# Batches 4 to 7: q transposed in 32x32 blocks by VectorE and moved by DMA, in place of TensorE transposes

## Chip, cores, metric

One core of a Trainium2 chip. The metric is the device time of one execution, in microseconds (us). A ratio is the mean time of one kernel's fast runs over that of the other's of the same rounds, so it is not quite the ratio of the medians quoted beside it.

## The reference, cut to what matters

```python
# attention without a score matrix; q, k, v: (8 batches, 8 heads, 576, 64)
q_s = softmax(q, axis=-1);  k_s = softmax(k, axis=2)
kv  = einsum('bhsd,bhse->bhde', k_s, v)
x   = einsum('bhsd,bhde->bhse', q_s, kv)       # -> (4608 tokens, 512)
# GEGLU block, d_ff = 1536
out = (gelu(x @ w_gate) * (x @ w_val)) @ w_out
```

## The kernel before

Per batch, TensorE runs the FFN of batch b (12 steps of four gate and four value matmuls, then four output tiles of twelve matmuls), and between these it prepares batch b+1. To multiply q by kv, q must lie with its features on the partitions, so it is transposed on TensorE into PSUM and copied back by VectorE. 512 of a batch's 576 tokens go through the FFN as one batch; the 64 left over of every batch are collected in `xtr` and run as a ninth, "left-over" batch between batches 6 and 7.

The names in the profile lines: `eq` is the exponential of q; `pst` and `pstr` are its transposes in PSUM (the memory that TensorE writes its results to), `eqt` the transposed q; `pskv` is the key-value product; `psx` and `psxr` are the products of kv with q for the 512 tokens and for the 64 left over, copied to `xt` and `xtr`; `psg` and `psv` are the results of the gate and value matmuls, `ht` is their gated product, `psy` an output tile.

```python
def unit_t(b, g, eng="dve"):                 # 8 transposes for two head pairs, 1 copy
    eqt = get_eqt(b)
    pst = ps_att.tile([P, 2, MAIN], f16, name="pst", tag="att")
    for j in range(2):
        hp = 2 * g + j
        for n in range(NM):
            nc.tensor.transpose(pst[:, j, n * P:(n + 1) * P],
                                eq_b[b % 2][:, n + 1, hp * P:(hp + 1) * P], ident)
    copy_on(eng, eqt[:, 2 * g:2 * g + 2, 0:MAIN], pst)
# unit_trem: the same for the 64 left-over tokens, 4 transposes, 1 copy

def unit_x(b, hp, eng="act", big=False):     # psx = kv^T q, copied to xt
    ...
def unit_xrem(b, eng="act"):                 # psxr, copied to xtr
    ...
def ffn_fi(xt, fi):                          # one FFN step
    psg = ps_big.tile([P, 512], f32, name="psg", tag="mm")   # ps_big: 6 PSUM buffers
    mm_gv(psg, wg_sb, xt, fi, range(HP))
    psv = ps_big.tile([P, 512], f32, name="psv", tag="mm")
    mm_gv(psv, wv_sb, xt, fi, range(HP))
    return gate(psg, psv)                    # gl = gelu(psg) on ScalarE; ht = psv*gl on VectorE
...
# what rides behind which FFN step (FI) or output tile (NS) of batch b, n = b + 1
at(b, FI, 0, L(norm, n, 0))
at(b, FI, 1, L(unit_kv, n, 0))
at(b, FI, 2, L(norm, n, 1))
at(b, FI, 3, L(unit_kv, n, 1))
at(b, FI, 4, L(unit_t, n, 0), L(norm, n, 2))
at(b, FI, 6, L(unit_x, n, 0), L(norm, n, 3))
at(b, FI, 7, L(unit_x, n, 1))
at(b, FI, 8, L(unit_t, n, 1))
at(b, FI, 9, L(unit_trem, n))
at(b, FI, 10, L(unit_x, n, 2), L(unit_x, n, 3))
at(b, FI, 11, L(unit_xrem, n))
```

The softmax here doesn't subtract the row's maximum and nothing guards it: scores larger than these inputs give would overflow.

## Time and profile before

| kernel before | |
|---|---|
| time, median of the first three runs | 328.32 us (328.05 to 328.36) |
| span of the profiled run | 325.9 us |
| TensorE busy | 98% of the span |
| VectorE, ScalarE, GpSimd busy | 55%, 45%, 13% |
| a batch that prepares the next / the left-over batch, which prepares none | 34.32 us / 31.08 us |

TensorE (PE) is the engine to read. Its matmuls are pipelined, so their durations overlap (a 512-column matmul shows 379 ns and starts every 216 ns); costs are read from the distance between starts. The lines are in the prediction.

### The profile page before, as it was taken

What the parts mean: (1) busy time and instruction counts of PE and PEld (TensorE: products, weight loads), DVE (VectorE), ACT (ScalarE), POOL (GpSimd) and SP (SyncE); (2) the same over time, 40 slices, a digit from 0 to 9 for tenths busy, and PEclk for the clock granted to TensorE, in tenths of its full rate; (3) what the DMA queues carried; (4) which work ended last, traced back from release to release, by engine and by line L of the source; (5) the groups of instructions that cost most, each with busy time, mean ns of one, the idle gap of its engine ahead of it and who ended that gap; (6) DMA issues with size and microseconds to landing.
All of it is one profiled execution on the core that took longest, in us unless ns stands there. A gap on an engine that the chain in (4) does not pass through costs nothing.

```text
span 325.9 us, 4574 instructions
## 1 busy us (share of the span) xinstructions
PE 320.4 (98%) x1750; PEld 155.4 (48%) x1750; DVE 180.2 (55%) x327; ACT 147.0 (45%) x197; POOL 43.9 (13%) x58
## 2 busy tenths in 40 slices
PE   8999999999999999999999999999999999999995
PEld 3544454445455445554455445544544444444444
DVE  2844376596589537952696249733983334323431
ACT  3663564989334662359224922484243033103310
POOL 1467451302003000030004000300000000000000
PEclk9999999999999999999999999999999999999999
DMA  7999999970196016801590049202100110041002
GB/s 227 364 383 394 402 392 392 392 264 0 69 321 224 2 65 231 319 0 46 169 391 10 0 142 379 94 0 85 45 2 0 64 64 2 0 103 27 1 33 97
DMA packets 38502, 50.49 MB, mean 155 GB/s; under 512 B 2128, under 2 KB 34256, under 8 KB 38480
## 3 DMA queue, kind: packets, MB, share of 16 engines
q1 hardware_dynamic: 38336, 50.14, 43.3%
q8 instruction: 13, 0.21, 0.2%
q10 hardware_dynamic: 144, 0.07, 0.1%
q14 instruction: 9, 0.07, 0.1%
HBM read 40.76 MB, written 9.44 MB: 154 GB/s over the span
## 4 chain that ended last, share of the span: by engine, by line
PE 94%; ACT 2%; issue 2%; DVE 1%; POOL 0%; POOLq 0%; ACTq 0%
PE psy L312 28%; PE psg L268 27%; PE psv L268 27%; PE pswarm L260 4%; PE pskv L194 3%; PE psx L246 2%; PE pst L219 2%; PE psl L333 1%; ACT L143 1%; ACT L273 1%; PE pstr L231 1%; DVE kv_sb L202 0%; ACT gl L273 0%; ACT eq L143 0%; PE psxr L253 0%
## 5 line engine op out<-in xcount | busy, mean ns | idle before, releaser
L273 ACT ACTIVATE gl<-psg 128x512 f32<-128x512 f32 x108 | 63.9, 598 | 137.5 <-PE psg L268 131.1
L275 DVE SCALAR_TENSOR_TENSOR ht<-psv,gl 128x512 f16<-128x512 f32 x108 | 73.9, 688 | 66.3 <-PE psv L268 64.3
L268 PE MATMUL psg<-xt,wg_sb 128*128 128x512 f16 x384 | 100.6, 379 | 0.1
L268 PE MATMUL psv<-xt,wv_sb 128*128 128x512 f16 x384 | 100.2, 379 | 0.1
L312 PE MATMUL psy<-wo_sb,ht 128*128 128x512 f16 x420 | 93.4, 379 | 0.0
L268 PEld LDWEIGHTS <-wv_sb 128*128 128x128 f16 x432 | 42.3, 98 | 51.7 <-issue 1.0
L312 PEld LDWEIGHTS <-ht 128*128 128x128 f16 x420 | 40.4, 98 | 46.9
L268 PEld LDWEIGHTS <-wg_sb 128*128 128x128 f16 x432 | 41.0, 98 | 44.2 <-issue 0.8
L361 DVE TENSOR_SCALAR yo<-psy 128x512 f32<-128x512 f32 x30 | 20.6, 689 | 48.8 <-PE psy L312 48.8
L119 POOL CAST v<-vt 128x640 f16<-128x640 f32 x26 | 19.1, 774 | 143.6 <-DMA vt<-in_v_dram 111.6
L160 DVE TENSOR_REDUCE rq<-eq 128x10 f32<-128x640 f16 (+1 forms) x32 | 25.3, 790 | 10.3 <-ACT eq L143 10.3
L167 DVE TENSOR_TENSOR eq<-eq,rrq 128x640 f16<-128x640 f16 (+1 forms) x28 | 23.6, 843 | 1.0
L121 ACT CAST xt<-psx 128x512 f16<-128x512 f32 x27 | 15.0, 587 | 16.4 <-PE psx L246 16.4
L143 ACT ACTIVATE eq<-qt 128x2560 f16<-128x2560 f32 (+1 forms) x9 | 18.3, 2049 | 4.5 <-DMA qt<-in_q_dram 4.4
L143 ACT ACTIVATE ek<-kt 128x2048 f16<-128x2048 f32 (+1 forms) x10 | 15.6, 1559 | 4.4 <-DMA kt<-in_k_dram 4.4
L260 PE MATMUL pswarm<-warm,ident 128*128 128x512 f16 x46 | 12.9, 445 | 1.4 <-POOL ident masks.py:199 1.4
L268 PE MATMUL psg<-xtr,wg_sb 128*128 128x512 f16 x48 | 12.3, 379 | 0.0
L268 PE MATMUL psv<-xtr,wv_sb 128*128 128x512 f16 x48 | 12.3, 379 | 0.0
L194 PEld LDWEIGHTS <-ek 128*128 128x128 f16 x160 | 10.3, 97 | 3.6 <-ACT v L121 0.4
L194 PE MATMUL pskv<-v,ek 128*128 128x130 f16 x160 | 11.8, 220 | 0.0
L246 PE MATMUL psx<-eqt,kv_sb 128*128 128x512 f16 x32 | 10.8, 381 | 0.3 <-DVE eqt L123 0.2
L143 ACT ACT_TABLE_LOAD x8 | 10.3, 1283 | 0.1
(56 smaller groups left out, 138.3 us busy)
## 6 DMA issues: line engine op xcount, KB each, us to landing
kt<-in_k_dram SPq DMA_DIRECT2D x14, 640.0 KB, 8.1
vt<-in_v_dram SPq DMA_DIRECT2D x14, 640.0 KB, 9.6
qt<-in_q_dram SPq DMA_DIRECT2D x14, 640.0 KB, 6.3
out_dram<-yo SPq DMA_DIRECT2D x14, 512.0 KB, 3.0
wost<-in_moe_w_out_dram SPq DMA_DIRECT2D x6, 512.0 KB, 8.6
wgst<-in_moe_w_gate_dram SPq DMA_DIRECT2D x5, 512.0 KB, 8.1
wvst<-in_moe_w_val_dram SPq DMA_DIRECT2D x5, 512.0 KB, 7.7
kt<-in_k_dram SPq DMA_DIRECT2D x4, 320.0 KB, 8.7
```

What stands on the lines that cost most here:

```text
L119: nc.gpsimd.tensor_copy(out=dst, in_=src)
L143: nc.scalar.activation(out=dst[:, c0:c1, h0 * D:h1 * D].rearrange("p n (h d) -> p h n d", d=D), in_=tiles[(nm, b)][:, h0:h1, c0 * D:c1 * D ...
L160: nc.vector.reduce_sum(rq, e, axis=mybir.AxisListType.X)
L167: (nc.gpsimd if eng == "pool" else nc.vector).tensor_tensor(out=e, in0=e, in1=rrq.unsqueeze(-1).to_broadcast((P, n, 2, D)), op=ALU.mult)
L194: nc.tensor.matmul(pskv[:, j, :], ek_b[b % 2][:, n, hp * P:(hp + 1) * P], v16_b[b % 2][:, n, 2 * hp:2 * hp + 2, 0:VW], start=(n == 0), sto ...
L246: nc.tensor.matmul(psx, st[(b, "kv", hp)].rearrange("p h e -> p (h e)"), st[(b, "eqt")][:, hp, 0:MAIN], start=True, stop=True)
L260: nc.tensor.matmul(ps, ident, warm, start=True, stop=True)
L268: nc.tensor.matmul(ps, w[:, ci, fi * P:(fi + 1) * P], xt[:, ci, :], start=(ci == 0), stop=(ci == HP - 1))
L273: nc.scalar.activation(out=gl, in_=psg, func=ACTF.Gelu)
L275: nc.vector.scalar_tensor_tensor(out=ht, in0=psv, scalar=_H_SCALE, in1=gl, op0=ALU.mult, op1=ALU.mult)
L312: nc.tensor.matmul(psy, hts[fi][:, ns * P:(ns + 1) * P], wo_sb[:, fi, :], start=(fi == 0), stop=(fi == NFI - 1))
L361: nc.vector.tensor_scalar(out=yo, in0=psy, scalar1=1.0 / _H_SCALE, scalar2=None, op0=ALU.mult)
```

## The change

The intent is to take the transposes off the engine that bounds the kernel. For batches 4 to 7 (`T32 = 4`) VectorE transposes each 32x32 block in place of the whole 128x128, and 16 small DMAs carry block (a, c) from partitions 32a to partitions 32c. With that, the products psx and psxr go from the FFN steps to between the output tiles, so that the moves have time to land. Two of the psx copies go from ScalarE to VectorE. The sums of the softmax of q (`norm_sum`) go from the FFN steps to the output tiles of the batch before. The block-transposed tile shares the weight-staging pool, whose buffers grow and go from eight to six.

```diff
-    wstp = ctx.enter_context(tc.tile_pool(name="wstp", bufs=8))
+    wstp = ctx.enter_context(tc.tile_pool(name="wstp", bufs=6))
...
+    def unit_t32(b, hp):
+        if (b, "et") not in st:
+            st[(b, "et")] = wstp.tile([P, HP, 4, NC * 32], f16, name="et", tag="wst")
+        et = st[(b, "et")]
+        nc.vector.transpose(
+            out=et[:, hp].rearrange("p c (n i) -> p n c i", i=32),
+            in_=eq_b[b % 2][:, :, hp * P:(hp + 1) * P].rearrange("p n (c j) -> p n c j", j=32))
+
+    def moves(b):
+        t = att.tile([P, HP * 4 * NC * 32], f16, name="eqt", tag="eqt").rearrange(
+            "p (h a x) -> p h a x", h=HP, a=4)
+        for a in range(4):
+            for c in range(4):
+                nc.sync.dma_start(out=t[32 * c:32 * c + 32, :, a, :],
+                                  in_=st[(b, "et")][32 * a:32 * a + 32, :, c, :])
+        t = t.rearrange("p h a (n i) -> p h n a i", i=32)
+        st[(b, "eqt5")] = t
...     (unit_x and unit_xrem read eqt5 where it is there)
+            if n < T32:
                 ...                       # as before
+            else:
+                for hp in range(HP):
+                    at(b - 1, NS, hp, L(norm_sum, n, hp))
+                    at(b, FI, hp, L(norm_mul, n, hp), L(unit_t32, n, hp))
+                at(b, FI, 4, L(moves, n))
+                at(b, FI, 5, L(unit_kv, n, 0))
+                at(b, FI, 7, L(unit_kv, n, 1))
+                at(b, NS, 1, L(unit_x, n, 0, "dve"), L(unit_x, n, 1, "dve"))
+                at(b, NS, 2, L(unit_x, n, 2, "act"), L(unit_x, n, 3, "act"))
+                at(b, NS, 3, L(unit_xrem, n))
```

More of the change, by code (lines that the diff above doesn't have):

```diff
@@ L108, with wst_tile @@
     wst = {}
+    ETW = HP * 4 * NC * 32
+    def wst_tile(name, n, w):
+        t = wstp.tile([P, ETW], f16, name=name, tag="wst")
+        return t[:, 0:2 * n * w].bitcast(f32).rearrange("p (n w) -> p n w", n=n)
     def load_w_gv(c):
         for w, nm in ((moe_w_gate, "wg"), (moe_w_val, "wv")):
-            t = wstp.tile([P, HP, WCH[c + 1] - WCH[c]], f32, name=f"{nm}st", tag="wst")
+            t = wst_tile(f"{nm}st", HP, WCH[c + 1] - WCH[c])
             nc.sync.dma_start(
@@ L129, in load_w_o @@
     def load_w_o(c):
-        t = wstp.tile([P, 2, C], f32, name="wost", tag="wst")
+        t = wst_tile("wost", 2, C)
         nc.sync.dma_start(
@@ L209, in get_eqt @@
         if (b, "eqt") not in st:
-            st[(b, "eqt")] = att.tile([P, HP, S], f16, name="eqt", tag="eqt")
+            st[(b, "eqt")] = att.tile([P, HP * 4 * NC * 32], f16, name="eqt", tag="eqt")[
+                :, 0:HP * S].rearrange("p (h t) -> p h t", h=HP)
         return st[(b, "eqt")]
@@ L235, in unit_trem, with xq, xqr @@
         nc.vector.tensor_copy(out=st[(b, "eqtr")], in_=pst[:, :, 0:REM] if b == 0 else pst[:, :, 0:P:2])
+    def unit_t32(b, hp):
[14 more added lines that the diff above has]
+        st[(b, "eqt5")] = t
+    def xq(b, hp):
+        if (b, "eqt5") in st:
+            return st[(b, "eqt5")][:, hp, 1:NC]
+        return st[(b, "eqt")][:, hp, 0:MAIN]
+    def xqr(b, hp):
+        if (b, "eqt5") in st:
+            return st[(b, "eqt5")][:, hp, 0, :, 0:32:2]
+        return st[(b, "eqtr")][:, hp, :]
     def get_xt(b):
@@ L246, in unit_x @@
         nc.tensor.matmul(psx, st[(b, "kv", hp)].rearrange("p h e -> p (h e)"),
-                         st[(b, "eqt")][:, hp, 0:MAIN], start=True, stop=True)
+                         xq(b, hp), start=True, stop=True)
         copy_on(eng, xt[:, hp, :], psx)
@@ L253, in unit_xrem @@
             nc.tensor.matmul(psx[:, hp, :], st[(b, "kv", hp)].rearrange("p h e -> p (h e)"),
-                             st[(b, "eqtr")][:, hp, :], start=True, stop=True)
+                             xqr(b, hp), start=True, stop=True)
         copy_on(eng, xtr[:, :, b * REM:(b + 1) * REM], psx)
@@ L460 @@
     at(2, NS, 2, L(unit_xrem, 0, "dve"))
+    T32 = 4
     for b in range(2, B):
@@ L466 @@
             n = b + 1
-            at(b, FI, 0, L(norm, n, 0))
-            at(b, FI, 1, L(unit_kv, n, 0))
-            at(b, FI, 2, L(norm, n, 1))
-            at(b, FI, 3, L(unit_kv, n, 1))
-            at(b, FI, 4, L(unit_t, n, 0), L(norm, n, 2))
-            at(b, FI, 6, L(unit_x, n, 0), L(norm, n, 3))
-            at(b, FI, 7, L(unit_x, n, 1))
-            at(b, FI, 8, L(unit_t, n, 1))
-            at(b, FI, 9, L(unit_trem, n))
-            at(b, FI, 10, L(unit_x, n, 2), L(unit_x, n, 3))
-            at(b, FI, 11, L(unit_xrem, n))
+            if n < T32:
+                at(b, FI, 0, L(norm, n, 0))
+                at(b, FI, 1, L(unit_kv, n, 0))
+                at(b, FI, 2, L(norm, n, 1))
+                at(b, FI, 3, L(unit_kv, n, 1))
+                at(b, FI, 4, L(unit_t, n, 0), L(norm, n, 2))
+                at(b, FI, 6, L(unit_x, n, 0), L(norm, n, 3))
+                at(b, FI, 7, L(unit_x, n, 1))
+                at(b, FI, 8, L(unit_t, n, 1))
+                at(b, FI, 9, L(unit_trem, n))
+                at(b, FI, 10, L(unit_x, n, 2), L(unit_x, n, 3))
+                at(b, FI, 11, L(unit_xrem, n))
+            else:
[8 more added lines that the diff above has]
+                at(b, NS, 3, L(unit_xrem, n))
     def ride(b, kind, i):
```

## The prediction

> **What bounds the kernel now.** I read the page's engine totals first, then the table by stage for single batches, then the timelines of TensorE and VectorE inside one batch, and last the DMA's own waits and landings.
>
> ```profile
> span 325.9 us, 4574 instructions
> ...
> PE 320.4 (98%) x1750; PEld 155.4 (48%) x1750; DVE 180.2 (55%) x327; ACT 147.0 (45%) x197; POOL 43.9 (13%) x58
> ...
> PE 94%; ACT 2%; issue 2%; DVE 1%; POOL 0%; POOLq 0%; ACTq 0%
> ```
>
> TensorE is busy for 98% of the span and carries 94% of the chain that ended last. A busy TensorE need not be a dense one, so the table by stage comes next; I cut it at the start of each batch's first gate matmul.
>
> ```profile
> core 0: us, PE busy (x) PEld busy (x) DVE busy (x) ACT busy (x) POOL busy (x), PEclk, DMA share, GB/s
> 122.60:156.93 34.33, 34.33 (x193) 16.89 (x192) 20.66 (x37) 16.98 (x22) 2.99 (x4) 1.00 0.41 146
> ...
> 225.59:259.90 34.31, 34.31 (x193) 16.88 (x192) 20.66 (x37) 9.78 (x17) 0.00 (x0) 1.00 0.08 31
> 259.90:290.98 31.08, 31.08 (x145) 14.07 (x144) 11.07 (x16) 7.16 (x12) 0.00 (x0) 1.00 0.13 38
> ```
>
> A batch that also prepares the next one takes 34.32 us; the batch of left-over rows, which prepares nothing, takes 31.08 us. There is no idle TensorE time in either, and the clock is full. The preparation thus costs 3.24 us of pure TensorE issue time. The TensorE timeline says what that is made of:
>
> ```profile
> 131.52 1.03 PE L268 MATMUL psv<-xt,wv_sb 128*128 128x512 f16 x4
> 132.39 0.61 PE L219 MATMUL pst<-ident,eq 128*128 128x128 f16 x8
> 132.83 1.03 PE L268 MATMUL psg<-xt,wg_sb 128*128 128x512 f16 x4
> ...
> 142.34 0.39 PE L231 MATMUL pstr<-ident,eq 128*128 128x128 f16 x4
> 142.57 1.03 PE L268 MATMUL psg<-xt,wg_sb 128*128 128x512 f16 x4
> ```
>
> The durations overlap; what counts is the distance between starts: 0.44 us for eight transposes (132.39 to 132.83), 0.23 us for the four of the remainder, so about 56 ns each. Twenty per batch are 0.45 + 0.45 + 0.23 = 1.12 us. The key-value products (2 x 0.57), the four 512-column products (4 x 0.216) and the four small ones (0.12) bring this to 3.24 us, which closes the account.
>
> **What the Trainium skill says.** "TensorE: Matmul & The Clock Gate", Back-to-back issue gap, gives 134 cycles, 56 ns at full clock, for 128 columns; the trace agrees. "VectorE: DVE Perf Modes", The three transpose paths, says that VectorE transposes 32x32 blocks only and lists 311 ns for 128x128 against 390 ns on TensorE. The 390 ns is no cost here: inside a dense stream the trace shows 56. "Vector Engine (DVE) Microarchitecture Reference", The reshape front end, says one element per cycle and lane for the transpose. Together these give my estimate for 640 elements: 311 ns plus 512 more elements at 0.96 GHz (533 ns), 0.84 us; the reduction over the same 640 elements took 0.81 us in the trace. "DMA: Bandwidth & Descriptors", Rules for kernel authors, says that transfers under 64 KB are mostly overhead; the 64 KB stores of the trace landed after 1.9 to 2.1 us, which fits.
>
> **The change, part by part.**
>
> *Removed.* For n = 4 to 7 (prepared during batches 3 to 6), 20 TensorE transposes each: 80 x 56 ns = 4.48 us, all on the path that sets the end. On VectorE two copies of 0.68 and one of 0.41 us per batch go (1.77 us).
>
> *Added on VectorE.* Four block transposes per batch, 4 x 0.82 = 3.3 us, and two of the four xt copies, formerly on ScalarE, 2 x 0.68. In all 20.66 - 1.77 + 3.3 + 1.4 = 23.6 us of a 33.2 us batch, so VectorE does not become the bound on average. Locally: it now does ht, multiply and transpose in each of the first four FFN steps. The timeline of before gives the spacing of such instructions:
>
> ```profile
> 124.60 0.69 DVE L275 SCALAR_TENSOR_TENSOR ht<-psv,gl 128x512 f16<-128x512 f32 x1 [1.11 <-PE psv L268]
> 125.21 0.81 DVE L160 TENSOR_REDUCE rq<-eq 128x10 f32<-128x640 f16 x1
> 126.05 0.22 DVE L162 RECIPROCAL rrq<-rq 128x10 f32<-128x10 f32 x1
> 126.31 0.83 DVE L167 TENSOR_TENSOR eq<-eq,rrq 128x640 f16<-128x640 f16 x1
> 127.05 0.68 DVE L275 SCALAR_TENSOR_TENSOR ht<-psv,gl 128x512 f16<-128x512 f32 x1
> ```
>
> ht to next 0.61, multiply to the transpose 0.87, transpose to next about 0.75: 2.23 us against the 1.73 us of an FFN step. VectorE falls back 0.5 us per step. The first Gelu is also later by some 0.5 us, because ScalarE's table load now comes after the last small copy. From the batch's start I get ht0 at 2.4, ht1 at 4.6, ht2 at 6.9, ht3 at 9.1, ht4 at 11.3 us. There are six PSUM buffers, that is three steps: the value matmuls of step 7 (at 13.5 us) need ht4 done (12.0), those of step 5 (9.5) need ht2 (7.55). The slack is 1.5 us or more, so TensorE doesn't wait. It would if a transpose took above roughly 1.2 us.
>
> *Added on DMA.* Sixteen moves of 40 KB per batch, in 320-byte pieces, issued after the last transpose (about 11.5 us into the batch), behind the six loads of batch b+2 on the same queue. In the instruction order each move waits for the transfer eight places earlier in that queue, so moves 3 to 8 wait for these loads.
>
> ```profile
> core 0: us, , PEclk, DMA share, GB/s
> ...
> 135.00:137.00 2.00, 1.00 0.99 365
> 137.00:139.00 2.00, 1.00 0.07 25
> ```
>
> The loads end near 137.3, that is 14.7 us into the batch. Ten moves are left then. The shortest issues on the queue in before (stores) took 0.54 us, so the last is issued near 14.7 + 5.4 = 20.1 and landed by about 22.5 us. The first psx that needs them now stands after the second output tile: 12 x 1.727 + 1.14 + 2 x 2.59 = 27.0 us. The margin is over 4 us; in batch 6, without loads, it is larger.
>
> *Moved.* All four psx and the psxr go from the FFN steps to between the output tiles. psx 2 and 3 wait for the PSUM buffers of 0 and 1, freed by VectorE about 1 us earlier than they are needed. ScalarE is done with its exponentials 6.0 us into the output tiles, before its first copy is due (8.6). In batches 3 to 5 nothing waits. But after batch 6 comes the batch of left-over rows, whose very first gate matmul reads xtr, and the last piece of xtr now comes from the psxr just before it. TensorE must wait for that copy:
>
> ```profile
> 249.43 0.28 PE L253 MATMUL psxr<-eqt,kv_sb 128*128 128x64 f16 x4
> ...
> 249.75 0.37 ACT L121 CAST xtr<-psxr 128x256 f16<-128x256 f32 x1 [0.38 <-PE psxr L253]
> ```
>
> 0.28 + 0.04 + 0.37 + 0.04 = 0.73 us from the first psxr, against 0.12 without a wait: 0.6 us lost, once.
>
> *Weight staging, six buffers for eight.* The weight loads in the first 45 us now wait for casts up to 0.8 us longer, but five transfers of 512 KB stay in flight (1.3 us each at 392 GB/s), so the queue stays full. I allow 0 to 0.3 us and take 0.
>
> Sum: 328.3 - 4.5 + 0.6 = **324.4 us**, 1.2% less.
>
> **Rivals.** (a) *The moves land late.* If an issue costs 1.2 us, as issues did while the queue was full at the start, ten take 12 us and the landing comes at about 29 us: TensorE would wait 2 us in each of batches 3, 4 and 5, and the time would be near 330. Against it: the queue is empty by then, and issues there took 0.54 to 0.59 us. (b) *VectorE holds PSUM.* With a transpose at half the assumed rate (1.5 us), ht4 ends near 14.8 us instead of 12.0 and TensorE loses some 1.3 us in each of four batches, which eats the whole gain: about 329.5. Against it speak the skill's rate and the reduction's 0.81 us. (c) *Hidden anyway.* If transposes were already covered, the time would stay at 328.3; the 34.32 against 31.08 us rules that out. (d) *The start stretches* through the two staging buffers less, by a microsecond at most: 325.5.
>
> **Range and chances.** The saving can't be above 4.5 us, so 2% (6.6 us) faster is out of reach unless the account of TensorE is wrong. The low end is the full saving with almost no wait, 323.3; the high end allows one rival at half strength, 327.5. Faster 0.02, same 0.93, slower 0.05; slower needs moves that are late by 4 us in every batch.
>
> **What would show it.** Right: TensorE has 80 instructions fewer, batches 3 to 5 take 33.2 us without idle TensorE time, batch 6 as much, and one wait of about 0.6 us for xtr stands ahead of the left-over batch. The block transpose reads 0.8 us, and the last move lands at least 3 us ahead of the first psx. Wrong: a wait of psx for a DMA (rival a), waits of psg or psv for VectorE in steps 5 to 8 (rival b), or a first batch that starts later (rival d).

## The result, and the profile after

324.36 us (median of 4 runs, 324.03 to 325.62) against 328.19 us (327.87 to 328.36): ratio 0.9892, interval 0.9864 to 0.9919. By the 2% mark that is "same"; it is clear of noise, and the predicted time was 324.4.

The page's totals of the changed kernel:

```profile
span 323.8 us, 4510 instructions
...
PE 315.9 (98%) x1670; PEld 150.9 (47%) x1670; DVE 189.9 (59%) x339; ACT 142.7 (44%) x189; POOL 43.1 (13%) x58
```

TensorE has 80 matmul records fewer (1750 to 1670) and is still 98% busy: it is still the bound, with less to do. The table by stage, again cut at each batch's first gate matmul (columns: stretch, its length, busy time of each engine with its instructions, clock, DMA share, GB/s):

```profile
core 0: us, PE busy (x) PEld busy (x) DVE busy (x) ACT busy (x) POOL busy (x), PEclk, DMA share, GB/s
124.40:157.61 33.21, 33.21 (x173) 15.77 (x172) 23.23 (x40) 14.27 (x18) 2.71 (x4) 1.00 0.51 171
...
224.04:257.87 33.83, 33.37 (x177) 15.81 (x175) 20.75 (x35) 10.27 (x17) 0.00 (x0) 1.00 0.17 51
257.87:288.95 31.08, 31.08 (x145) 14.09 (x145) 10.52 (x16) 7.16 (x12) 0.00 (x0) 1.00 0.13 38
```

A preparing batch takes 33.21 us in place of 34.32 to 34.33, 1.11 us less, with TensorE dense in it. Batch 6 takes 0.62 us more than its fellows, with 0.46 us of idle TensorE. TensorE's waits in the whole run, longest first (total, times, longest):

```profile
engine line waited for: us in total, times, longest us
PE pskv L200 <- DVE v L129: 1.9, 1, 1.9
...
PE psg L305 <- ACT xtr L127: 0.5, 1, 0.5
```

There is no wait for a move and none of the FFN for VectorE. The second line is the predicted one, seen here in TensorE's timeline: 0.74 us from the first psxr to the gate matmul, where 0.73 had been worked out.

```profile
257.13 0.28 PE L290 MATMUL psxr<-eqt,kv_sb 128*128 128x64 f16 x4
257.87 1.02 PE L305 MATMUL psg<-xtr,wg_sb 128*128 128x512 f16 x4 [0.46 <-ACT xtr L127]
```

VectorE's timeline in the first FFN step of batch 3, in place of the reduce, reciprocal and multiply shown before:

```profile
126.40 0.69 DVE L312 SCALAR_TENSOR_TENSOR ht<-psv,gl 128x512 f16<-128x512 f32 x1
127.00 0.81 DVE L173 TENSOR_TENSOR eq<-eq,rrq 128x640 f16<-128x640 f16 x1
127.85 0.85 DVE L249 STREAM_TRANSPOSE et<-eq 128x640 f16<-128x640 f16 x1
128.62 0.65 DVE L312 SCALAR_TENSOR_TENSOR ht<-psv,gl 128x512 f16<-128x512 f32 x1
```

One transpose of 640 elements takes 0.845 us, a step 2.22 us. The DMA queue's issues, and the first product that needs the moves:

```profile
129.12 2.15 SPq L103 DMA_DIRECT2D vt<-in_v_dram  x2
135.31 11.55 SPq L258 DMA_DIRECT2D eqt<-et  x16
```

```profile
151.45 0.59 PE L283 MATMUL psx<-eqt,kv_sb 128*128 128x512 f16 x2
```

The last of the sixteen issues runs from 146.26 to 146.86. A move lands 2.0 us (median) after its issue, counted from the start of the issue. The last one so lands at 148.2, or 3.2 us before psx starts at 151.45; in batches 4, 5 and 6 it lands 3.9, 3.0 and 3.9 us before.

**The start of the profiled run.** The 1.9 us wait in the list of waits is not part of the change's mechanism. In this one run (325.62 us, the slowest of the four) the first k and v loads landed late (the last of v at 15.4 us instead of 13.7), before any staging buffer is used a second time (16.8 us), and batch 3 started at 124.40 us instead of 122.60. It hides in the span what the change does. So I compare the stretch from batch 3's first gate matmul to the end of the span, which does not contain the start:

| profiled run | batch 0's first gate matmul | batch 3 starts | span | from batch 3 to the end |
|---|---|---|---|---|
| before | 17.42 | 122.60 | 325.9 | 203.3 |
| six staging buffers alone (e3) | 17.77 | 122.99 | 326.3 | 203.3 |
| transposes put back (e1) | 18.11 | 123.43 | 327.3 | 203.9 |
| changed | 19.07 | 124.40 | 323.8 | 199.4 |
| changed, no moves (e2) | 17.81 | 123.28 | 322.7 | 199.4 |
| changed, early psxr of batch 7 (e4) | 18.54 | 123.64 | 322.4 | 198.8 |

Before to changed: 3.9 us less, which is 80 x 56 ns minus the 0.6 us. The first column shows that the runs differ before batch 0's FFN begins: from there to batch 3 it is 105.1 to 105.5 us in all six.

### The profile page after: what moved, and what is told of

Its sections match the earlier page's. It is cut to its first block, busy times and chain, and to the rows that moved or that the text cites. A ratio compares the mean times of both kernels' runs of the same rounds, so it can differ in the third digit from the quotient of the medians.

```text
span 323.8 us, 4510 instructions
## 1 busy us (share of the span) xinstructions
PE 315.9 (98%) x1670; PEld 150.9 (47%) x1670; DVE 189.9 (59%) x339; ACT 142.7 (44%) x189; POOL 43.1 (13%) x58
## 4 chain that ended last, share of the span: by engine, by line
PE 86%; ACT 3%; DMA 3%; issue 2%; DVE 2%; SPq 1%; POOL 0%; DVEq 0%; ACTq 0%; POOLq 0%
PE psg L305 27%; PE psv L305 27%; PE psy L349 26%; DMA vt<-in_v_dram 3%; PE pskv L200 3%; PE psx L283 2%; ACT L149 1%; SPq L103 1%; ACT eq L149 1%; PE psl L370 1%; ACT L310 1%; PE pst L226 1%; DVE kv_sb L208 0%; DVE rq L166 0%; ACT gl L310 0%
## 5 line engine op out<-in xcount | busy, mean ns | idle before, releaser
L312 DVE SCALAR_TENSOR_TENSOR ht<-psv,gl 128x512 f16<-128x512 f32 x108 | 73.0, 683 | 66.7 <-PE psv L305 62.3
L349 PE MATMUL psy<-wo_sb,ht 128*128 128x512 f16 x420 | 94.7, 379 | 0.0
L125 POOL CAST v<-vt 128x640 f16<-128x640 f32 x26 | 18.3, 743 | 141.8 <-DMA vt<-in_v_dram 108.4
L166 DVE TENSOR_REDUCE rq<-eq 128x10 f32<-128x640 f16 (+1 forms) x32 | 25.3, 791 | 10.4 <-ACT eq L149 10.0
L127 ACT CAST xt<-psx 128x512 f16<-128x512 f32 x19 | 10.3, 588 | 27.3 <-PE psx L283 27.3
L249 DVE STREAM_TRANSPOSE et<-eq 128x640 f16<-128x640 f16 x16 | 13.5, 845 | 0.6
```

Of the source, the lines that this page charges most:

```text
L125: nc.gpsimd.tensor_copy(out=dst, in_=src)
L166: nc.vector.reduce_sum(rq, e, axis=mybir.AxisListType.X)
L249: nc.vector.transpose(out=et[:, hp].rearrange("p c (n i) -> p n c i", i=32), in_=eq_b[b % 2][:, :, hp * P:(hp + 1) * P].rearrange("p n (c ...
L312: nc.vector.scalar_tensor_tensor(out=ht, in0=psv, scalar=_H_SCALE, in1=gl, op0=ALU.mult, op1=ALU.mult)
L349: nc.tensor.matmul(psy, hts[fi][:, ns * P:(ns + 1) * P], wo_sb[:, fi, :], start=(fi == 0), stop=(fi == NFI - 1))
```

## The experiments

The first four ran together on one chip, 5 rounds; before had 328.11 us (327.75 to 329.08) there.

**e1: the transposes put back as dead work.**

```diff
-                at(b, FI, 4, L(moves, n))
+                at(b, FI, 4, L(moves, n), L(dummy_t, n, 0))
+                at(b, FI, 8, L(dummy_t, n, 1))
+                at(b, FI, 9, L(dummy_trem, n))       # transposes into PSUM, no copy
```

> The changed kernel, with the twenty TensorE transposes of each of batches 4 to 7 put back as dead work beside the moves (their PSUM result is read by nobody). Theory (the gain is the issue time of 80 transposes at 56 ns): 324.3 + 4.5 = 328.8 us, a batch from 33.2 back to 34.3 us. Rival (the gain comes from moving the products between the output tiles, or from what left VectorE and ScalarE): it stays near 324.3 us. Anything in between splits the gain.

Measured: 329.01 us (328.57 to 330.11), ratio to before 1.0024 (1.0008 to 1.0041). A batch is back at 34.34 us:

```profile
123.43:157.77 34.34, 34.34 (x194) 16.83 (x193) 23.23 (x40) 14.27 (x18) 2.72 (x4) 1.00 0.50 165
```

VectorE's busy time in it is the 23.23 us of the changed kernel, and the products still stand between the output tiles; only the transposes are back, and with them the 1.13 us. So the gain is their issue time. The rest of the change by itself costs something: this kernel is slower than before, in the table above by 0.6 us, the wait for xtr.

**e2: the moves left out** (a result that is wrong: blocks stay on their partitions).

```diff
-                at(b, FI, 4, L(moves, n))
+                at(b, FI, 4, L(nomoves, n))          # eqt5 = a view of et, no DMA
```

> The changed kernel without the sixteen moves; the products read the block-transposed tile where it lies, so the result is wrong on purpose. Theory (the moves land before they are needed, with 2.6 us to spare in the profile): the same 324.3 us within 0.3. Rival (the moves cost TensorE time somewhere, by late landing or by slowing the loads): faster than 324.0 us, by up to what they cost.

Measured: 324.18 us (323.92 to 324.49), and 199.4 us from batch 3 to the end, the same as with the moves. They cost TensorE nothing. (The 2.6 us of this expectation, and of that of e6, counted the landing from the end of the issue; it is 3.2 us.) A side result: this kernel passed the comparison with the reference, although its q blocks are misplaced. The inputs have a standard deviation of 0.1, so all weights of the softmax over 64 features are near 1/64, and which row of q is used barely shows. A pass therefore says little about the moves; that block (a, c) reaches partitions 32c I checked in the indices only.

**e3: the kernel before with six staging buffers.**

```diff
-    wstp = ctx.enter_context(tc.tile_pool(name="wstp", bufs=8))
+    wstp = ctx.enter_context(tc.tile_pool(name="wstp", bufs=6))
```

> The kernel before with six weight-staging buffers for eight and nothing else changed. Prediction: 328.2 us, at most 0.3 more. Rival (the start stretches; in the profile of the changed kernel the DMA moved 233 GB/s at 16 to 18 us, where the kernel before had 384): 328.7 to 330 us, and the first gate matmul of batch 3 later than 122.6 us by as much. The profiled run of the changed kernel had it 1.8 us later, but there the very first k and v loads had landed late, before any staging buffer is used again.

Measured: 328.13 us (327.86 to 329.94), ratio 1.0009 (0.9987 to 1.003). The interval leaves room for no cost above 0.3% (1 us), and the DMA at 16 to 18 us moved 382 GB/s. Batch 3 did start 0.39 us later than before, but 0.35 us of that stood already at batch 0's first gate matmul, after TensorE had waited 0.52 us for v; from there to batch 3 it took 105.22 us, and 105.18 before. The dip to 233 GB/s belonged to the late start of the changed kernel's run. (The opposite trial, the changed kernel with eight of its larger buffers, does not build: SBUF is too small.)

**e4: the wait for xtr taken away.**

```diff
-                at(b, NS, 2, L(unit_x, n, 2, "act"), L(unit_x, n, 3, "act"))
-                at(b, NS, 3, L(unit_xrem, n))
+                if n < B - 1:
+                    ...                              # as above
+                else:
+                    at(b, NS, 2, L(unit_x, n, 2, "act"), L(unit_xrem, n))
+                    at(b, NS, 3, L(unit_x, n, 3, "act"))
```

> The changed kernel, where batch 7 alone computes its left-over product after the third output tile of batch 6 and its fourth 512-column product after the fourth. Theory (0.74 us between psxr and the first gate matmul of the left-over batch, against 0.12 without a wait): 0.6 us faster than the changed kernel, 323.7 us, and no wait for xtr in the trace. Rival (TensorE would wait there anyway for something else): unchanged 324.3 us.

Measured: 323.66 us (323.21 to 324.22), ratio to before 0.986 (0.9843 to 0.9877); 198.8 us from batch 3 to the end, 0.6 less than the changed kernel. TensorE's timeline has no wait left there:

```profile
256.27 0.38 PE L283 MATMUL psx<-eqt,kv_sb 128*128 128x512 f16 x1
256.49 1.03 PE L305 MATMUL psg<-xtr,wg_sb 128*128 128x512 f16 x4
```

The next three ran together; before had 328.59 us (327.67 to 329.21).

**e5: the better version, from batch 3 on.**

```diff
-    T32 = 4
+    T32 = 3
-    at(2, NS, 2, L(unit_xrem, 0, "dve"))
+    at(2, NS, 3, L(unit_xrem, 0, "dve"))
     (and the edit of e4)
```

> The early left-over product of batch 7 as in the run before, and the new path for batch 3 too (prepared in batch 2); the left-over product of batch 0 goes from after the third output tile of batch 2 to after the fourth, so that it doesn't take a PSUM buffer that the fourth 512-column product needs. Theory (56 ns for each transpose taken off TensorE, nothing else): 100 transposes instead of 80, 324.3 - 0.6 - 1.1 = 322.6 us. Rival (VectorE and ScalarE are fuller in batch 1's output tiles, where the norm sums of batch 3 now fall): 323.5 us or more, with a wait of TensorE in batch 2.

Measured: 322.66 us (322.24 to 322.89), ratio to before 0.9822 (0.9799 to 0.9844), with no wait in batch 2. From batch 2's first gate matmul to the end the profiled run took 232.7 us instead of 238.3: 5.6 us less, which is 100 x 56 ns. It beats both kernels: its slowest run lies below the changed kernel's fastest (324.03).

**e6: the moves cut in two.**

```diff
+                for h in (0, 2):
-                nc.sync.dma_start(out=t[32 * c:32 * c + 32, :, a, :],
-                                  in_=st[(b, "et")][32 * a:32 * a + 32, :, c, :])
+                    nc.sync.dma_start(out=t[32 * c:32 * c + 32, h:h + 2, a, :],
+                                      in_=st[(b, "et")][32 * a:32 * a + 32, h:h + 2, c, :])
```

> The changed kernel with each move cut into two of half the size: 32 per batch, the same bytes. In the profile sixteen moves took 10.4 to 11.6 us to issue, about 0.65 us each, and landed 2.0 us later. Theory (the time of the moves is that of their issues, and they had 2.6 us to spare): the last lands about 10.9 + 32 x 0.65 + 2.0 = 33.7 us into the batch, the first product needs it at 27.05, so TensorE waits 6.6 us in each of four batches: about 351 us; with 0.56 us for the smaller ones 339 us. Rival (the moves take their time from the bytes or from the loads ahead of them): the landing hardly moves and the time stays within 1 us of 324.3.

Measured: 355.57 us (353.11 to 357.09), a little over the range. The queue and TensorE in batch 3:

```profile
130.90 25.21 SPq L259 DMA_DIRECT2D eqt<-et  x32
```

```profile
145.24 5.34 PE L350 MATMUL psy<-wo_sb,ht 128*128 128x512 f16 x24
156.74 1.04 PE L284 MATMUL psx<-eqt,kv_sb 128*128 128x512 f16 x2 [6.17 <-DMA eqt<-et]
157.57 5.13 PE L350 MATMUL psy<-wo_sb,ht 128*128 128x512 f16 x12
```

With the same bytes and twice the DMAs, the issuing took 25.2 us instead of 11.6 (about 1.8 us of it a wait: the first half-size move needs only two of the four block transposes and goes out early, the second waits for the rest). Issues follow each other 0.64 us apart at either size: the moves cost their issues, not their bytes. The wait of 6.17 us is near the 6.6 expected; the four batches together waited 21.4 us. What I had left out is the line after it: twelve matmuls of the output tile took 5.13 us, where they take 2.75 in the changed kernel. The clock (third number from the end of each row) shows why:

```profile
core 0: us, PE busy (x) PEld busy (x) DVE busy (x) ACT busy (x) POOL busy (x), PEclk, DMA share, GB/s
154.00:155.00 1.00, 0.00 (x0) 0.00 (x0) 0.00 (x0) 0.00 (x0) 0.00 (x0) 1.00 0.17 38
...
159.00:160.00 1.00, 1.00 (x4) 0.31 (x3) 0.62 (x2) 0.00 (x0) 0.00 (x0) 0.50 0.00 0
...
163.00:164.00 1.00, 1.00 (x6) 0.47 (x5) 1.00 (x2) 1.00 (x2) 0.00 (x0) 1.00 0.00 0
```

"TensorE: Matmul & The Clock Gate" (The HAM clock gate) says that an idle window of about 3.4 us brings the array to half its clock; this trace agrees, with half the clock from 155.55 us, 5.0 us after the last matmul, to 162.38. So these waits cost more than their length: batch 3 lost 6.3 us to the wait and 2.8 us to the half clock after it. Waits of up to 2.0 us (e8, below) left the clock at 1.00; where between the two the loss begins, no run here shows.

**e7 and e8: every block transpose done two or three times.**

```diff
+        for _ in range(2):        # e8: range(3)
-        nc.vector.transpose(
+          nc.vector.transpose(
```

> The changed kernel with every block transpose of VectorE done twice into the same place. The extra 0.77 us makes a step of 2.95 us against TensorE's 1.73. Theory (three steps of PSUM buffers are all the slack that TensorE has against VectorE): ht4 would be done about 15.0 us into the batch, the value matmuls of step 7 want it at 13.5: about 1.5 us of waiting in each of four batches, 330 us (327 to 333), the wait at steps 6 and 7. Rival (VectorE, busy 60% of the span, has room for 12 us more): 324.3 us.

Measured: 324.86 us (324.08 to 325.27). My number was wrong: 13.5 us more of VectorE work cost nothing that can be told from noise, and TensorE has no wait for VectorE in the FFN. The two timelines of batch 3 contradict the model directly. VectorE starts ht4 here (the first of the two):

```profile
137.54 1.25 DVE L313 SCALAR_TENSOR_TENSOR ht<-psv,gl 128x512 f16<-128x512 f32 x2
```

and the value matmuls of step 7 had started before it:

```profile
136.78 1.03 PE L306 MATMUL psv<-xt,wv_sb 128*128 128x512 f16 x4
```

The PSUM buffers (banks) that the built program gives to each tile say why; no trace shows them. Six PSUM buffers are not handed around in a ring of three steps. Each new tile gets, at build time, one that the builder takes to be free first. Gate tiles, read early by ScalarE, come back after two or three steps and are used again; value tiles, which wait for VectorE, are left alone for four. In the changed kernel the gate tile of step 8 takes the bank of value tile 4 (ht4); with the doubled transposes value tile 8 takes it, and value tile 7 that of value tile 3. That is four steps of slack. I ran the threefold version (3 rounds, before 328.19 us, 327.88 to 329.52) to test this:

> Every block transpose three times. The twofold run cost nothing, and the built program says why the model of three steps was wrong: PSUM buffers are given out at build time in the order in which they are freed there, and the value matmuls of step k take the buffer of the value matmuls of step k-4 (before: the gate matmuls of step k take it), not k-3. Revised theory (four steps): with steps of 2.18 + 2 x 0.87 = 3.93 us on VectorE, ht3 is done at 14.95 us into the batch, and the value matmuls of step 7 want it at 13.5: 1.45 us of waiting, then 1.6 us for ht4 at step 8, about 3.0 us per batch; the moves start at 18.3 us and land at 30.7, another 0.6 us. In four batches 12 to 14 us: 336 to 339 us. Rival (VectorE never holds TensorE here, as its busy share is still under 90% in a batch): 324.5 us. With the old model of three steps it would be some 3 us more per batch: about 350 us.

Measured: 338.9 us (338.21 to 340.28), inside the revised range. TensorE waits for ht twice in each of the four batches, 12.1 us of idle time in all, and at the steps named. The four batches took 36.08 to 37.42 us, together 14.5 us more than in the changed kernel. In batch 3:

```profile
137.59 1.02 PE L306 MATMUL psv<-xt,wv_sb 128*128 128x512 f16 x4 [0.89 <-DVE ht L313]
...
141.53 1.02 PE L306 MATMUL psv<-xt,wv_sb 128*128 128x512 f16 x4 [1.48 <-DVE ht L313]
```

## Why the prediction was right, point by point

- **The saving (4.48 us): right.** Shown by e1, which gives it back, and by the batch length of 33.21 us. The step that carried it was the closed account of one batch: 34.32 minus 31.08 equals the parts. With TensorE dense, what is removed from it is removed from the time.
- **The wait for xtr (0.6 us, once): right.** 0.74 us against a computed 0.73; e4 takes it away and gains it.
- **VectorE is no bound: right, with a wrong term.** The transpose (0.845 us against an estimated 0.84) and the step (2.22 against 2.23) came as estimated. The slack was mis-sized: "six PSUM buffers, that is three steps" is four steps in the built program, as e7 and e8 show. The error was on the safe side: the reason given for "TensorE doesn't wait" was wrong, the conclusion held. The threshold that I gave, some 1.2 us for a transpose, was too low: 1.7 us (twofold) is free, 2.6 us (threefold) costs 14.5 us. The choice of buffer can be read from the build, before any run.
- **The moves land in time: right, with less to spare.** I had 22.5 us into the batch and a margin of over 4 us. In batch 3 the last landed 23.8 us in (148.2 minus 124.40), with 3.2 us to spare; the least of the four batches is 3.0, just at the "at least 3 us" that was to show it right. Two terms were too small: the last load of v landed 16.7 us into the batch, not 14.7, and the issues came 0.64 us apart, not 0.54. The whole sixteen took 11.55 us from 10.9 us on, 1.2 us of it waiting. e2 shows that nothing of it reaches TensorE; e6 shows how near the edge it is.
- **The staging buffers (0 us): right.** e3 shows no cost within its interval, and its trace 0.04 us from batch 0's first gate matmul to batch 3. The stretched start of the profiled run looked like rival (d); it was there before a staging buffer is used again. Why the first loads of v land up to 1.7 us apart from run to run stays open.
- **The range:** its low end of 323.3 us, "the full saving with almost no wait", is 0.5 us below 328.3 - 4.5 = 323.8; the prediction does not say where that comes from.

## What to carry to other kernels

Where one engine is dense, find a batch that lacks the work in question and close the account of the difference; its issue time is then what removing it gains, and put-back dead work proves it. Moving work to idle engines is free only up to a slack that is set by buffers and by the issue time of small DMAs, so measure that slack by doing the new work two and three times before relying on it. Look for the one place where the moved work's last piece is the next stage's first input: here it gave back 0.6 of 4.5 us and cost three lines to mend.

## What the Trainium skill lacked or had wrong

- "VectorE: DVE Perf Modes", The three transpose paths, compares TensorE's 390 ns with VectorE's 311 ns for 128x128. In a dense TensorE stream the transpose costs 56 ns (eight in 0.44 us), and VectorE took 0.845 us for 128x640, that is 169 ns for each 128x128. Here single durations did not tell which path is cheaper; the engine that bounds the kernel did.
- "DMA: Bandwidth & Descriptors", Issuing engines are not separate DMA queues, calls the time to initiate a DMA usually small beside the DMA itself. Here it set when the last move landed: issues from one queue came 0.64 us apart at 40 KB and at 20 KB, so that sixteen took 10.4 to 11.6 us, and 32 with the same bytes 23.7 to 25.3 us.
- No page has how PSUM buffers are reused in a built program: with six buffers and two tiles per step, the slack towards the slower reader was four steps, not three (twofold transposes 324.86 us, threefold 338.9 us).
